# Fixing 512-row blocks of the two common experts early and running them, and the last pair of token blocks, in the wide form

## The chip, the core and the metric

The kernel runs on one core of a Trainium2 chip. The metric is device time in microseconds, from three runs of the program: 732.78, 734.6 and 736.45 us, median 734.6 us. A core has a matrix engine (PE) with its own weight loader (PEld), a vector engine (DVE), a scalar engine (ACT), a general engine (POOL) and SyncE (SP). In this kernel POOL also issues the indirect DMAs, which scatter and gather rows, and SP issues the plain DMAs.

## The reference

Three layers follow one another over 2304 tokens (4 batches of 576) of width 512, in float32.

```python
scores = where((rel >= 0) & (rel < 64), q @ k.T / 8, -1e9)      # window of 64, 8 heads of 64
x = softmax(scores) @ v                                         # 2304 x 512
h = x @ w_in                                                    # 512 -> 2048
x = (h * tanh(log1p(exp(h)))) @ w_out                           # 2048 -> 512
logits = x @ w_gate + modality_bias[modality_id]                # 8 experts
e_idx, gate_w = argmax(logits), softmax(logits)[e_idx]
out[token] = gate_w * (relu(x[token] @ w1[e_idx]) @ w2[e_idx])  # 512 -> 1024 -> 512
```

Which expert a token takes is known only when the kernel runs. With these inputs two of the eight experts get all tokens: 1168 and 1136 of the 2304. After six of the nine token blocks they hold 764 and 772.

## The kernel before

**Precision.** Each float32 matrix product is made as three products of parts: an operand is split in a high part (a rounded copy, by ACT) and a low part (the rest, a subtraction, by DVE), and high·high, low·high and high·low are summed in PSUM. So each tile of weights and of activations costs one ACT and one DVE instruction before PE can use it.

**Steps.** After a start in which the attention is alone, the main loop of `tile_kernel` runs 112 steps. A step makes one piece of hidden values (`hidden`, `hidden_wide` or `hidden_rows`) and, by `out_step(i - LAG)` with LAG = 2, the output products of the piece made two steps earlier. The text below numbers the steps from 0.

- Steps 0 to 47 are *wide* token steps. The list `WIDE = 0, 2, 4` names pairs of blocks of 256 tokens. `hidden_wide` multiplies 128 hidden columns with 512 tokens, 12 matmuls of 512 columns (L372 to L374), and `output_wide` makes 12 matmuls of 512 columns (L418 to L420). A pair takes 16 steps.
- Steps 48 to 71 are *narrow* token steps for blocks 6, 7 and 8, 8 steps each. `hidden` takes 256 hidden columns and 256 tokens: 24 matmuls of 256 columns (L356, L359, L360). `output` makes 12 matmuls of 512 columns (L407 to L409).
- Steps 72 to 103 are eight blocks of 256 rows of one expert each, 4 steps a block, narrow like the token steps. Three of them (`EARLY = 3`) are of the commonest expert and are fixed before the last tokens are routed; five (`FULL = 5`) come from a table.
- Steps 104 to 111 are two remainder slots, of 160 and of 128 rows, with `hidden_rows`. The 32 rows over 128 (`FEW = 32`) of the first are computed apart by `few_x`, `few_hidden`, `few_turn`, `few_output`, in steps 100 to 103.
- Further slots stand in conditional code at the end (`ns > 0`). With these inputs none of them runs.

**Between the layers.** A token step's hidden values pass through the activation: `mish_a` and `mish_b` on ACT and DVE, then `split_g`; an expert step's through `relu`. A finished token block is copied out of PSUM by `keep_rows`, and then routed in small tasks that are taken from a list, up to two a step: `route_logits` (DVE, L627, 16 dot products a block), `choose`, `weigh`, `place`. `place` makes five 8-column matmuls (L678 to L682), finds each row's place in a table by expert in DRAM, and scatters the 256 rows there by two indirect DMAs of POOL (L706). After four blocks `pick` finds the commonest expert; after seven, `cut` fixes its first 768 rows. After the ninth, `table` computes the slots of all other rows.

**Expert rows.** `gather` (L981, POOL) fetches 128 rows of the table, and must wait for the scatters. `turn` transposes them on PE (L1004) and splits them (ACT L1008, DVE L1009). At a block's end `finish` scales each 128 rows out of PSUM (ACT L1081) and scatters them into the output by an indirect DMA of POOL (L1082). These DMAs write the same tensor, and each one waits until the one before has landed.

**Expert weights** come by SP in pieces of 1 MB (`fetch_w`) and are split in parts of 128x1024 (`split_w1` L966 and L967, `split_w2` L974 and L975), each 1024-column part by one ACT and one DVE instruction.

**Order.** The schedule is manual: each engine runs its instructions in the order in which the code issues them, so a PE instruction that waits holds up all PE work after it, and a POOL DMA that waits holds up the gathers and scatters behind it.

Of the kernel before, what the change touches and what calls it, by code (L numbers as in the profile page):

```python
# [11 lines left out]
F32 = mybir.dt.float32  # L12
F32R = mybir.dt.float32r
BF16 = mybir.dt.bfloat16
# [38 lines left out]
EARLY = 3  # L53
# [11 lines left out]
WAIT = 1  # L65
TURN_AT = 71
NO_TASKS = 31, 47
# [217 lines left out]
class Rounds:  # L285


    def __init__(self, nc, ctx, tc, a):
        self.nc, self.tc, self.ctx = nc, tc, ctx
        self.a = a  # L290
        self.c = {}
        self.s1, self.s2, self.x01, self.home = [], [], None, None
# [219 lines left out]
    def route_consts(self):  # L512
# [67 lines left out]
        def last():  # L580
# [10 lines left out]
            nc.vector.tensor_scalar(lanes[:, FULL, 1:2], oi[:, 1:2], float(P), None, ALU.add)  # L591
# [128 lines left out]
    def pick(self):  # L720
# [3 lines left out]
        cnt = k.tile([P, NE], F32, name="cnt0")  # L724
        nc.vector.tensor_tensor(cnt, c["base"], c["r8"], ALU.subtract)
        m8 = k.tile([P, NE], F32, name="pick_m")
        i8 = k.tile([P, NE], U32, name="pick_i")
        nc.vector.max(out=m8, in_=cnt)
        nc.vector.max_index(out=i8, in_max=m8, in_values=cnt)
        c["e0i"] = i8  # L730
        c["e0"] = k.tile([P, 1], F32, name="e0")
        nc.vector.tensor_copy(c["e0"], i8[:, 0:1])
        c["first"] = k.tile([P, NE], F32, name="first")
        nc.vector.tensor_scalar(
            c["first"], c["e8"], c["e0"], float(EARLY * G), ALU.is_equal, ALU.mult
        )

        c["start"] = k.tile([P, NE], F32, name="start1")
        nc.vector.tensor_tensor(c["start"], c["r8"], c["first"], ALU.add)
        d = k.tile([P, 16], F32, name="d16")  # L740
        w = c["w16"] = k.tile([P, 16], F32, name="w16")
        nc.vector.tensor_scalar(d, c["i16"], c["e0"], None, ALU.subtract)
# [3 lines left out]
    def cut(self):  # L746

        nc, c = self.nc, self.c
        k = self.k_pool
        cnt = k.tile([P, NE], F32, name="cnt1")  # L750
        nc.vector.tensor_tensor(cnt, c["base"], c["r8"], ALU.subtract)
        nc.vector.tensor_tensor(cnt, cnt, c["first"], ALU.mult)
        n0 = k.tile([P, 1], F32, name="n0")
        nc.vector.tensor_reduce(out=n0, in_=cnt, op=ALU.add, axis=AX.X)
        nc.vector.tensor_scalar(n0, n0, 1.0 / (EARLY * G), None, ALU.mult)
        off = k.tile([P, 1], F32, name="off0")
        nc.vector.tensor_scalar(off, c["e0"], float(RCAP), float(-SENT), ALU.mult, ALU.add)
        n = 2 * EARLY
        valid = k.tile([P, n], F32, name="valid0")
        nc.vector.tensor_scalar(valid, c["lane"], n0, None, ALU.is_lt)  # L760
        t = k.tile([P, n], F32, name="idx0f")
        nc.vector.scalar_tensor_tensor(t, c["lane"], off, valid, ALU.add, ALU.mult)
        c["idx0"] = k.tile([P, n], I32, name="idx0")
        nc.vector.tensor_scalar(c["idx0"], t, float(SENT), None, ALU.add)
        nc.vector.tensor_tensor(c["base"], c["base"], c["start"], ALU.max)

    def table(self):
# [12 lines left out]
        def room(tag):  # L780
            pl = self.m_pool if tag == "y" else self.m1_pool
            t = pl.tile([P, 2 * G], F32, name="room", tag=tag)
# [12 lines left out]
        def counts():  # L795

            tmp = room("y")
# [17 lines left out]
            big = room("pq")(4 * Q * Q // 2).bitcast(BF16)  # L815
# [14 lines left out]
        def counts2():  # L830
# [27 lines left out]
            ts(at[:, 0:1], last(1), float(FULL), None, ALU.max)  # L858
# [5 lines left out]
            nc.vector.tensor_copy(q[:, :FULL], c["i16"][:, 0:FULL])  # L864
            nc.vector.tensor_copy(q[:, FULL:], at)
            nc.vector.tensor_copy(more, c["i16"][:, FULL : FULL + NSLOT - STRAIGHT])
# [4 lines left out]
            stt(has[:, 0:1], total, float(-FULL), has[:, 0:1], ALU.add, ALU.subtract)  # L871
# [5 lines left out]
        def part(lo, n, q):  # L877
# [5 lines left out]
            def experts():  # L883
                ind = st["ind"] = room("r")(n, 4 * Q + 1)
                tmp = st["tmp"] = room("pq")
# [92 lines left out]
    def gather(self, idx, i):  # L978

        r = self.row_pool.tile([P, ROW], F32, name="grow", tag=f"row{i % 2}")  # L980
# [12 lines left out]
    def gather_slot(self, s):  # L993
        idx = self.c["idx"].rearrange("p s t -> p (s t)")
        return [self.gather(idx, 2 * s + t) for t in range(1 if s == STRAIGHT - 1 else 2)]

    def turn(self, rows):
        nc = self.nc
        x = self.x_tile()
# [44 lines left out]
    def few_output(self, i):  # L1044
        nc = self.nc
        if i == 0:
            self.facc = self.acc_ps.tile([P, P], F32, name="few", tag="acc1")
# [51 lines left out]
def tile_kernel(tc, a):  # L1099
    nc = tc.nc  # L1100
    with ExitStack() as ctx:
# [22 lines left out]
        with tc.manual_schedule():  # L1124
# [144 lines left out]
            def wait_early():  # L1269
                late.extend((lambda: None,) * WAIT)  # L1270
                for s in range(EARLY):
                    rows[s] = []
                    for t in range(2):
                        late.append(lambda s=s, t=t: rows[s].append(R.gather(c["idx0"], 2 * s + t)))

            def first_slot():
                rows[EARLY] = R.gather_slot(0)
# [311 lines left out]
```

## Time and profile before

| what | value |
|---|---|
| runs, median (lowest to highest) | 734.6 us (732.78 to 736.45) |
| the profiled execution | 734.63 us, of which the span (first to last instruction) 732.8 us |
| PE busy | 710.3 us, 97% of the span |
| DVE busy | 563.4 us, 77% |
| ACT busy | 497.0 us, 68% |
| POOL busy | 153.6 us, 21% |
| granted PE clock, mean | 0.993 |

The span is 1.8 us shorter than the execution; what lies around it is in neither kernel's code. Busy time of PE is the sum of its matmuls' durations as the profile models them, with overlaps of neighbours counted once. Since a matmul's modelled duration reaches into the next one, the pace at which matmuls start is a second reading beside their duration, and the two can differ.

### The profile page before, as it was taken

Reading aid. Unit: us, or ns where it says so; the run is one execution under the profiler, and the core shown is the slowest. Engines: PE = TensorE matmul, PEld = TensorE weight load, DVE = VectorE, ACT = ScalarE, POOL = GpSimd, SP = SyncE. Lnnn points to the kernel's source line nnn. Section 1 sums busy time; section 2 is a strip of 40 time slices with the busy share of each in tenths; the row PEclk is TensorE's granted clock in tenths of the full one; section 3 lists DMA queues with packets and bytes.
Section 4 is the critical chain, followed back from the end, with each engine's and each line's share of the span. In section 5 each row is a group of like instructions: output and inputs, shape, how many; then the busy total and the mean of one; then the engine's idle time right before and its main releaser. Section 6 shows DMA issues by size and latency. Waiting matters only on the chain. (4 is left out here: it accounts for less than half of the span.)

```text
span 732.8 us, 13083 instructions
## 1 busy us (share of the span) xinstructions
PE 710.3 (97%) x4613; PEld 611.1 (83%) x4613; DVE 563.4 (77%) x1355; ACT 497.0 (68%) x1045; POOL 153.6 (21%) x292
## 2 busy tenths in 40 slices
PE   6879999999999999999999999999999999999996
PEld 5767878888888888888898899998999899999885
DVE  4879998976555479999999999998889665555562
ACT  4978888899776678777777777776322555554572
POOL 4762233232223010101101101041022112201111
PEclk9999999999999999999999999999999999999998
DMA  9986666752231331000000000360011721101350
GB/s 260 300 257 200 222 198 225 232 145 81 80 94 43 130 95 53 29 1 30 29 1 30 15 16 30 116 229 31 1 58 59 251 65 58 47 27 44 123 184 30
DMA packets 43884, 75.45 MB, mean 103 GB/s; under 512 B 3809, under 2 KB 22241, under 8 KB 43682
## 3 DMA queue, kind: packets, MB, share of 16 engines
q1 hardware_dynamic: 31842, 56.01, 24.3%
q0 software_dynamic: 4432, 14.46, 5.7%
q10 hardware_dynamic: 7536, 4.06, 1.9%
q8 instruction: 38, 0.62, 0.4%
q14 instruction: 36, 0.29, 0.1%
HBM read 82.36 MB, written 13.19 MB: 130 GB/s over the span
## 5 line engine op out<-in xcount | busy, mean ns | idle before, releaser
L627 DVE CUSTOM_DVE_ANT_0 junk<-row,wg 128x512 bf16<-128x512 f32 x144 | 99.2, 689 | 2.7
L477 ACT ACTIVATE y<-h 128x512 f32<-128x512 f32 x72 | 43.1, 598 | 55.6 <-PE h L374 32.5
L218 POOL TENSOR_SCALAR p<-p,r 128x128 f32<-128x128 f32 x144 | 68.2, 490 | 59.9 <-DVE r L211 56.2
L418 PE MATMUL acc<-w,g 128*128 128x512 f32 x192 | 77.8, 405 | 0.0
L420 PE MATMUL acc<-w,g 128*128 128x512 f32 x192 | 75.1, 391 | 0.0
L419 PE MATMUL acc<-w,g 128*128 128x512 f32 x192 | 74.8, 390 | 0.0
L504 ACT ACTIVATE g<-h 128x512 fp32r<-128x512 f32 x32 | 19.1, 598 | 80.3 <-PE h L360 80.3
L359 PE MATMUL h<-x,ew 128*128 128x256 f32 x256 | 72.6, 284 | 0.7 <-DVE x L1009 0.6
L356 PE MATMUL h<-x,ew 128*128 128x256 f32 x256 | 72.7, 284 | 0.0
L360 PE MATMUL h<-x,ew 128*128 128x256 f32 x256 | 72.4, 283 | 0.0
L488 ACT ACTIVATE pq<-pq,mid 128x512 f32<-128x512 f32 x72 | 52.3, 726 | 20.4 <-DVE pq L482 15.7
L482 DVE SCALAR_TENSOR_TENSOR pq<-y,r 128x512 f32<-128x512 f32 x72 | 49.6, 688 | 19.9 <-ACT r L480 19.3
L497 DVE TENSOR_TENSOR g<-y,g 128x512 fp32r<-128x512 f32 x72 | 49.5, 687 | 18.9 <-ACT g L496 18.7
L967 DVE TENSOR_TENSOR ew<-s,ew 128x1024 fp32r<-128x1024 f32 x32 | 39.2, 1224 | 31.8 <-ACT ew L966 31.7
L706 POOL DMA_INDIRECT xs_dram<-row,posi x18 | 18.6, 1034 | 208.4 <-DVE pq L489 69.5
L489 DVE SCALAR_TENSOR_TENSOR pq<-pq,r 128x512 f32<-128x512 f32 x72 | 50.2, 698 | 12.3 <-ACT pq L488 12.2
L407 PE MATMUL acc<-ew,g 128*128 128x512 f32 x144 | 57.9, 402 | 0.0
L408 PE MATMUL acc<-ew,g 128*128 128x512 f32 x144 | 56.4, 392 | 0.0
L409 PE MATMUL acc<-ew,g 128*128 128x512 f32 x144 | 56.2, 390 | 0.0
L478 ACT ACTIVATE y<-y,half 128x512 f32<-128x512 f32 x72 | 52.2, 725 | 2.4
L490 DVE SCALAR_TENSOR_TENSOR y<-pq,h 128x512 f32<-128x512 f32 x72 | 49.5, 687 | 3.8
L1082 POOL DMA_INDIRECT out<-out,grow x18 | 19.0, 1055 | 153.2 <-ACT out L1081 132.3
(277 smaller groups left out, 2115.3 us busy)
## 6 DMA issues: line engine op xcount, KB each, us to landing
s<-e_w SPq DMA_DIRECT2D x32, 1024.0 KB
v<-v SPq DMA_DIRECT2D x36, 256.0 KB
raw<-w_in SPq DMA_DIRECT2D x16, 512.0 KB
raw<-w_out SPq DMA_DIRECT2D x16, 512.0 KB
kt<-kT SPq DMA_DIRECT2D x17, 384.0 KB
qd<-qT SPq DMA_DIRECT2D x36, 128.0 KB
x_dram<-xs ACTq DMA_DIRECT2D x14, 256.0 KB
xraw<-x_dram SPq DMA_DIRECT2D x10, 256.0 KB
```

Of the source, the lines that this page charges most:

```text
L218: nc.gpsimd.tensor_scalar(p[:, c, :], p[:, c, :], r[:, c : c + 1], 0.0, ALU.mult, ALU.add)
L356: nc.tensor.matmul(h[:, f], w[:, 0, k, fs], xh[k], start=(k == 0), stop=False)
L359: nc.tensor.matmul(h[:, f], w[:, 0, k, fs], xl[k], start=False, stop=False)
L360: nc.tensor.matmul(h[:, f], w[:, 1, k, fs], xh[k], start=False, stop=(k == KD - 1))
L407: nc.tensor.matmul(acc[c], gh[:, 0, f, cs], w[:, 0, f], start=st, stop=False)
L408: nc.tensor.matmul(acc[c], gh[:, 0, f, cs], w[:, 1, f], start=False, stop=False)
L409: nc.tensor.matmul(acc[c], gh[:, 1, f, cs], w[:, 0, f], start=False, stop=en)
L418: nc.tensor.matmul(acc[c], gc[:, 0], w[:, 0, f], start=first, stop=False)
L419: nc.tensor.matmul(acc[c], gc[:, 0], w[:, 1, f], start=False, stop=False)
L420: nc.tensor.matmul(acc[c], gc[:, 1], w[:, 0, f], start=False, stop=last)
L488: nc.scalar.activation(p, p, AF.Square, bias=self.c["mid"][:, 0:1])
L627: nc.vector.tensor_tensor_reduce(out=junk, in0=rows[c][:, 0:D], in1=self.wg[:, e], scale=1.0, scalar=0.0, op0=ALU.mult, op1=ALU.add, accum ...
```

## The change

- Blocks 6 and 7 become a fourth wide pair (`WIDE = 0, 2, 4, 6`). Its four 512-token pieces of input are split late in step 47, as `HOMES[6]` says.
- `pick` runs twice and finds the two commonest experts. `cut` runs after block six's routing and again after all nine, and each time fixes 512 rows of both. These are four blocks of 512 rows, in the order `SLOT_EXPERT = 0, 1, 1, 0`, with a step kind of their own, "e": 8 steps a block, `hidden_wide` and `output_wide`.
- The table of slots keeps only the two remainder slots (`STRAIGHT = 2`), again of 160 and 128 rows.
- A wide block has four groups of 128 rows, and so four transposes in a block's last two steps (`turn_part`), four scalings and four output DMAs at its end. `finish` puts every other scaled piece in buffers of `x_pool`.
- Rows that wait longer are kept in `stash_pool`. The weights of both experts are fetched and split by a hand-written plan (`ADVANCE`, `experts_step`). 40 parts are split where before there were 64, since a wide block shares its weights with twice as many rows.
- The routing tasks are taken by a rate (`RATE`), one dot product as one task.

```diff
-EARLY = 3
+EARLY = 4
...
-NSLOT = 17
+NSLOT = 16
...
-STRAIGHT = 7
-FULL = 5
+STRAIGHT = 2
...
-CUT_AFTER = 6
-DOTS = 2, 2, 2, 2, 2, 2, 2, 2
+CUTS = {6: 0, NG: 1}
...
+SLOT_EXPERT = 0, 1, 1, 0
+ADVANCE = (
+    ((0, 1, 2),),
+    ((0, 2, 0),),
+    ((0, 1, 3),),
+    ((0, 2, 1), (1, 1, 0)),
+    ((0, 2, 2), (1, 1, 1)),
+    ((0, 2, 3), (1, 2, 0)),
+    ((1, 1, 2), (1, 2, 1)),
+    ((1, 2, 2),),
+)
+RATE = (0, 2), (70, 1), (72, 2), (80, 3)
...
-WIDE = 0, 2, 4
+WIDE = 0, 2, 4, 6
...
+    6: (("xraw", 0, -1, False), ("xh", 0, -1, False), ("xh", 1, -1, False), ("xl", 0, -1, False)),
...
+    def homes(self, b):
+        shape = [P, KD, 2 * G]
+        if b % 2 == 0:
+            return [self.w2_pool.tile(shape, F32R, name="ex", tag="w2") for _ in range(2)]
+        return [self.xs_pool.tile(shape, F32R, name="ex", tag=tag) for tag in ("xh", "xl")]
+
+    def turn_part(self, home, rows, t):
...
+            nc.tensor.transpose(ps[:, k], rows[:, k * P : (k + 1) * P], self.c["ident"])
+        xh, xl = (x[:, :, t * P : (t + 1) * P] for x in home)
+        nc.scalar.copy(xh, ps)
+        nc.vector.tensor_tensor(xl, ps, xh.bitcast(F32), ALU.subtract)
...
     def finish(self, acc, rows):
         nc = self.nc
         for t in range(len(rows)):
-            y = self.m_pool.tile([P, D], F32, name=f"out{t}", tag="y")
+            if t % 2:
+                y = self.x_pool.tile([P, D], F32, name=f"out{t}", tag="xraw")
+            else:
+                y = self.m_pool.tile([P, D], F32, name=f"out{t}", tag="y")
...
-            NS = EARLY + STRAIGHT
+            NS = NE_W + STRAIGHT
             steps += [("w", b, j) for b in WIDE for j in range(2 * FP)]
             steps += [("m", b, j) for b in range(WIDE[-1] + 2, NG) for j in range(FP)]
-            steps += [("s", s, k) for s in range(NS) for k in range(FS)]
+            steps += [("e", s, k) for s in range(NE_W) for k in range(2 * FS)]
+            steps += [("s", s, k) for s in range(NE_W, NS) for k in range(FS)]
...
+            def gather_early(s, t):
+                stash = s == 1 and t >= 2 or s == 3
+                idx = R.early[s // 2][:, SLOT_EXPERT[s]]
+                return R.gather(idx, t, R.stash_pool if stash else R.row_pool)
...
+                if b == 1 and j == 1:
+                    for i in range(2):
+                        R.fetch_w(e0, None, 2, i)
+                        R.fetch_w(e0, None, 1, i)
...
+                if (b, j) in ((1, 3), (2, 2)):
+                    rows[b + 1] = [gather_early(b + 1, t) for t in range(4)]
...
+                elif part == "e":
+                    xh, xl = xsp[part, b]
+                    x = [(xh[:, k], xl[:, k]) for k in range(KD)]
+                    h = R.hidden_wide(ew1[b, j // 2], j % 2, x)
...
+                if part == "e" and j >= 6 and b + 1 < NE_W:
+                    turn_two(b + 1, j - 6)
```

**Order on PE, first expert step (step 72).** In the kernel before these are the last three of its 24 hidden matmuls and the first three of its 12 output products (`x` is the turned rows, `ew` the first expert's w1 parts, `acc` and `w` the last token block's):

```order
L356 MATMUL h<-x,ew_5878 128x256
L359 MATMUL h<-x,ew_5878 128x256
L360 MATMUL h<-x,ew_5878 128x256
L407 MATMUL acc_5590<-w_1892,g 128x512
L408 MATMUL acc_5590<-w_1892,g 128x512
L409 MATMUL acc_5590<-w_1892,g 128x512
```

In the changed kernel these are the last three of its 12 hidden matmuls (`ex` is the rows' home) and the first four of the 12 output products of the last token block:

```order
L385 MATMUL h<-ex,ew_5643 128x512
L386 MATMUL h<-ex,ew_5643 128x512
L387 MATMUL h<-ex,ew_5643 128x512
L420 MATMUL acc_5390<-w_1892,g 128x512
L421 MATMUL acc_5390<-w_1892,g 128x512
L422 MATMUL acc_5390<-w_1892,g 128x512
L420 MATMUL acc_5391<-w_1892,g 128x512
```

The hidden matmuls have 512 columns instead of 256, and half as many weight loads stand between them; the output products are the same.

**Order on DVE, after the routing of block 3 (steps 51 to 53).** Before, `pick` stands in one piece (L725 to L744; `cnt` are the counts by expert, `e` the expert found), ahead of the two operations that end the hidden values of the step (L489, L490):

```order
L725 TENSOR_TENSOR cnt_4579<-base,r_3241 128x8
L728 MAX pick_m<-cnt_4579 128x8
L729 MAX_INDEX pick_i<-pick_m,cnt_4579 128x8
L732 CAST e_4585<-pick_i 128x1
L734 TENSOR_SCALAR first<-e_3237,e_4585 128x8
L739 TENSOR_TENSOR start_4589<-r_3241,first 128x8
L742 TENSOR_SCALAR d_4591<-i_3296,e_4585 128x16
L743 TENSOR_SCALAR w_4592<-d_4591 128x16
L744 SCALAR_TENSOR_TENSOR w_4592<-d_4591,w_4592 128x16
L489 SCALAR_TENSOR_TENSOR pq<-pq,r 128x512
L490 SCALAR_TENSOR_TENSOR y<-pq,h 128x512
```

Now the two picks stand each in a task of its own (L738 to L760), and the first comes after such an L502, L503 pair (L489, L490 of before):

```order
L503 SCALAR_TENSOR_TENSOR y<-pq,h 128x512
L738 TENSOR_TENSOR cnt_p_4553<-base,r_3241 128x8
L745 MAX pick_m_4555<-cnt_p_4553 128x8
L746 MAX_INDEX pick_i_4556<-pick_m_4555,cnt_p_4553 128x8
L749 CAST e_4559<-pick_i_4556 128x1
L751 TENSOR_SCALAR own_4561<-e_3237,e_4559 128x8
L753 TENSOR_SCALAR off_4563<-e_4559 128x1
L758 TENSOR_SCALAR d_4565<-i_3296,e_4559 128x16
L759 TENSOR_SCALAR w_4566<-d_4565 128x16
L760 SCALAR_TENSOR_TENSOR w_4566<-d_4565,w_4566 128x16
L495 SCALAR_TENSOR_TENSOR pq<-y,r 128x512
L510 TENSOR_TENSOR g<-y,g 128x512
```

Nine small operations ahead of the activation became nine and later seven, with L495, the activation's first multiplication, and L510, the low part of `g`, between.

**Order on POOL, after the first expert block.** Before, the scatters of block 7's tokens (`row_5551`), the two output DMAs of the first 256 rows, the scatters of block 8's tokens (`row_6130`), and the first gathers from the table:

```order
L706 DMA xs_dram<-row_5551,posi 24577x514
L704 MEMSET apart 128x1
L706 DMA xs_dram<-row_5552,posi 24577x514
L1082 DMA out<-out_6375,grow 2304x512
L1082 DMA out<-out_6380,grow 2304x512
L706 DMA xs_dram<-row_6130,posi 24577x514
L704 MEMSET apart 128x1
L706 DMA xs_dram<-row_6131,posi 24577x514
L981 DMA grow<-xs_dram,idx 128x514 x2
```

Now the four output DMAs of the first 512 rows, the scatters of block 8's tokens (`row_5881`) and the four gathers of the third block's rows, which need what was just scattered:

```order
L1126 DMA out<-out_6292,grow 2304x512
L1126 DMA out<-out_6297,grow 2304x512
L1126 DMA out<-out_6302,grow 2304x512
L1126 DMA out<-out_6307,grow 2304x512
L719 DMA xs_dram<-row_5881,posi 26625x514
L717 MEMSET apart 128x1
L719 DMA xs_dram<-row_5882,posi 26625x514
L1005 DMA grow<-xs_dram,idx_6389 128x514 x4
```

Between the first output DMA and the first gather behind it stand five other DMAs instead of three, and four of the outputs follow one another.

## Rows read from the trace of the kernel before

**Rows 1.** The page's part 1: busy time, share of the span and instructions of each engine.

```profile
PE 710.3 (97%) x4613; PEld 611.1 (83%) x4613; DVE 563.4 (77%) x1355; ACT 497.0 (68%) x1045; POOL 153.6 (21%) x292
```

**Rows 2.** Time line of PE, a wide and a narrow step: start us, us, instruction.

```profile
303.50 0.39 PE L372 MATMUL h<-xw,w 128*128 128x512 f32 x1
303.73 0.39 PE L373 MATMUL h<-xw,w 128*128 128x512 f32 x1
...
308.94 0.39 PE L372 MATMUL h<-xw,w 128*128 128x512 f32 x1
...
421.36 0.28 PE L356 MATMUL h<-x,w 128*128 128x256 f32 x1
421.48 0.28 PE L359 MATMUL h<-x,w 128*128 128x256 f32 x1
...
426.98 0.28 PE L356 MATMUL h<-x,w 128*128 128x256 f32 x1
```

**Rows 3.** Groups by line and shape, PE: busy us, mean ns, idle before.

```profile
L372 PE MATMUL h<-xw,w 128*128 128x512 f32 x128 | 51.1, 399 | 0.0
...
L356 PE MATMUL h<-x,w 128*128 128x256 f32 x160 | 45.5, 284 | 0.0
```

**Rows 4.** Windows of steps 48 to 63, 72 to 103: length, engines' busy, PEclk, DMA.

```profile
363.80:455.30 91.50, 91.17 (x592) 81.97 (x591) 85.96 (x251) 67.23 (x119) 6.10 (x9) 1.00 0.05 18
...
501.90:695.30 193.40, 192.72 (x1356) 174.31 (x1352) 129.54 (x261) 90.16 (x132) 33.86 (x33) 1.00 0.21 71
```

**Rows 5.** Time line of PE: first matmuls of steps 52 to 55; one of step 84.

```profile
386.45 0.36 PE L356 MATMUL h<-xw,w 128*128 128x256 f32 x1
...
392.47 0.36 PE L356 MATMUL h<-xw,w 128*128 128x256 f32 x1 [0.16 <-DVE y L490]
...
398.17 0.28 PE L356 MATMUL h<-xw,w 128*128 128x256 f32 x1
...
404.17 0.39 PE L356 MATMUL h<-xw,w 128*128 128x256 f32 x1 [0.18 <-DVE y L490]
...
573.48 0.39 PE L359 MATMUL h<-x,ew 128*128 128x256 f32 x1 [0.57 <-DVE x L1009]
```

**Rows 6.** Time line of DVE in step 52: the pick's first operation, what follows it.

```profile
388.90 0.16 DVE L725 TENSOR_TENSOR cnt<-base,r 128x8 f32<-128x8 f32 x1
...
390.89 0.72 DVE L489 SCALAR_TENSOR_TENSOR pq<-pq,r 128x512 f32<-128x512 f32 x1
391.64 0.69 DVE L490 SCALAR_TENSOR_TENSOR y<-pq,h 128x512 f32<-128x512 f32 x1
```

**Rows 7.** Time line of ACT, a block's end in step 106.

```profile
703.87 1.27 ACT L1081 ACTIVATE out<-acc,grow 128x512 f32<-128x512 f32 x2
705.84 0.39 ACT L387 ACTIVATE hrow<-h 128x256 f32<-128x256 f32 x1 [0.69 <-PE t L394]
```

**Rows 8.** Time line of POOL: issues of indirect DMAs.

```profile
538.31 1.00 POOL L1082 DMA_INDIRECT out<-out,grow  x1 [30.67 <-ACT out L1081]
541.84 0.99 POOL L1082 DMA_INDIRECT out<-out,grow  x1 [2.54 <-ACT g L504]
543.14 1.40 POOL L706 DMA_INDIRECT xs_dram<-row,posi  x1 [0.30 <-issue]
...
557.25 1.09 POOL L981 DMA_INDIRECT grow<-xs_dram,idx  x1 [11.44 <-DVE g L505]
558.64 1.19 POOL L981 DMA_INDIRECT grow<-xs_dram,idx  x1 [0.30 <-issue]
...
585.18 1.02 POOL L1082 DMA_INDIRECT out<-out,grow  x1 [14.98 <-ACT out L1081]
590.17 1.36 POOL L1082 DMA_INDIRECT out<-out,grow  x1 [3.96 <-DMA out<-out,grow]
```

**Rows 9.** Line L706, the scatters: from issue to landing.

```profile
DMA to landing us min/median/max: 2.9/4.0/5.3
```

**Rows 10.** Line L981, the gathers: from issue to landing.

```profile
DMA to landing us min/median/max: 3.3/3.8/8.0
```

More of the change, by code (lines that the diff above doesn't have):

```diff
@@ L728, in pick @@
         nc.vector.max(out=m8, in_=cnt)
         nc.vector.max_index(out=i8, in_max=m8, in_values=cnt)
[L730 to L739, printed above, removed]
+        c[f"e{i}i"] = i8
@@ L743, in pick, with cut @@
         nc.vector.tensor_scalar(w, d, float(NE), None, ALU.is_lt)
         nc.vector.scalar_tensor_tensor(w, d, 0.0, w, ALU.is_ge, ALU.mult)
-    def cut(self):
+    def cut(self, i, lo, hi):
         nc, c = self.nc, self.c
         k = self.k_pool
[L750 to L765, printed above, removed]
@@ new lines, in cut @@
+        cnt = k.tile([P, 3, NE], F32, name=f"cnt_c{i}")
+        n = k.tile([P, 2], F32, name=f"n{i}")
+        nc.vector.tensor_tensor(cnt[:, 2], c["base"], c["r8"], ALU.subtract)
+        for w in range(2):
+            nc.vector.tensor_tensor(cnt[:, w], cnt[:, 2], c[f"own{w}"], ALU.mult)
+        nc.vector.tensor_reduce(out=n, in_=cnt[:, 0:2], op=ALU.add, axis=AX.X)
+        lane = c["lane"][:, lo:hi]
+        start, was = k.tile([P, NE], F32, name=f"start{i}"), c["r8"]
+        for w in range(2):
+            nc.vector.scalar_tensor_tensor(
+                start, c[f"own{w}"], float(hi * P), was, ALU.mult, ALU.add
+            )
+            was = start
@@ L795, in counts @@
         def counts():
-            tmp = room("y")
+            tmp = room("row0")
             n = tmp(Q)
@@ L870, in counts2 @@
             tt(has[:, 0:1], has[:, 0:1], has[:, 1:2], ALU.add)
-            stt(has[:, 0:1], total, float(-FULL), has[:, 0:1], ALU.add, ALU.subtract)
+            tt(has[:, 0:1], total, has[:, 0:1], ALU.subtract)
             c["ns"] = k.tile([P, 1], I32, name="ns")
@@ L1380, in start_mish, with pull @@
                     mish = R.mish_a(h)
+            def pull(at):
+                if at >= len(tasks):
+                    return []
+                if isinstance(tasks[at], list):
+                    return tasks.pop(at)
+                n = [rate for first, rate in RATE if first <= i][-1]
+                now = []
+                while len(now) < n and at < len(tasks) and not isinstance(tasks[at], list):
+                    now.append(tasks.pop(at))
+                return now
             def run_tasks():
@@ L1387, in run_tasks @@
                     route_block(*waiting.pop(0))
-                now = tasks.pop(0) if tasks else []
-                if not now and waiting and waiting[0][0] < NG - 1:
+                now = pull(0)
+                if not now and waiting:
+                    at = len(tasks)
                     route_block(*waiting.pop(0))
-                    now = tasks.pop(1)
+                    now = pull(at)
                 if late:
@@ L1420, in change_x, with turn_two, split_one @@
                         xsp["m", b] = R.split_x(b == WIDE[-1] + 2)
+            def turn_two(b, half):
+                if half == 0:
+                    xsp["e", b] = R.homes(b)
+                assert len(rows[b]) == 4
+                for t in (2 * half, 2 * half + 1):
+                    R.turn_part(xsp["e", b], rows[b][t], t)
+            def split_one(s, what, k):
+                if what == 1:
+                    ew1[s, k] = R.split_w1(k)
+                else:
+                    ew2[s, k] = R.split_w2(k)
```

230 lines of the change are left out of this document (136 added, 94 removed).

## The prediction

> **What bounds the kernel now.** I read the page first: PE is busy for 97% of the span, the other engines far less [rows 1]. So what counts is how fast PE can issue its matmuls, and where it waits. For the pace I went to the time line of PE and read the starts, not the durations. In a wide step the hidden matmuls start 0.23 us apart and the next step begins 5.44 us after the last; in a narrow step they start 0.12 us apart and the step takes 5.62 us [rows 2]. The grouping by shape gives another picture: a 256-column matmul has a mean of 284 ns, a 512-column one 399 ns [rows 3]. By those means 1152 narrow matmuls would cost 327 us and 576 wide ones 230 us, a gain of 97 us. But a duration reaches beyond the next start, so the durations overlap and cannot be added; the starts decide.
>
> Then the stages. The windows of steps 48 to 63 (blocks 6 and 7) and of 72 to 103 (expert blocks) show PE busy all but 0.3 and 0.7 us, at a granted clock of 1.00, that is 2.4 GHz [rows 4]. The clock has nothing to give, and PE hardly waits. The waits that exist I looked for at step starts: steps 52, 53 and 54 take 6.02, 5.70 and 6.00 us instead of 5.62, and two of them begin or end with PE waiting for DVE's L490; one wait of 0.57 us for L1009 stands in step 84 [rows 5].
>
> **Width.** The change turns 16 token steps (48 to 63) and 32 expert steps (72 to 103) from narrow to wide. Each step does the same products. The 12 output matmuls are equal in both forms, only the hidden part differs. From the step starts [rows 2]: 5.62 - 5.44 = 0.18 us a step, 48 x 0.18 = **-8.6 us**, all of it on PE's path. Turns (72 transposes), small products for the 32 extra rows and remainder slots are as many as before: nothing.
>
> The Trainium skill, "TensorE: Matmul & The Clock Gate", section "Back-to-back issue gap", gives an isolated gap of N/2.4 + 2.5 ns. By it two 256-column matmuls take 218.3 ns and a 512-column one 215.8, which would save 2.5 ns a pair, 1.4 us in all. The rows show 0.12 and 0.23 us starts, and by whole steps 15 ns a pair, so the sum goes by the rows; the rule's result is a rival below.
>
> **Waits in the token steps.** In step 52 the routing of block 3 and `pick` stand in one piece on DVE: `pick` alone runs from 388.90 to 390.89, and only then come L489 and L490, which free the hidden values' buffer for step 53 [rows 6]. PE waits 0.16 us there [rows 5]. The three steps lose 0.86 us against 5.62, of which routing's small matmuls take some. In the changed order L502 and L503 come ahead of the pick, and the two picks are apart. This can give back 0.86 us at most; what the two smaller pieces delay is still there, so less is likely. Against it, step 47 now splits four pieces of input, not two: two more ACT and DVE operations like L490, 0.69 us each, 1.4 us if nothing hides them. What hides them is that L490's result is waited for only in the clump of step 52. I take -0.6 us, with ends of -0.9 and +1.4.
>
> **Waits in the expert steps.** The 0.57 us wait in step 84 [rows 5] comes behind a burst of weight splits in steps 82 and 83, and goes. In its place the splits for both experts lie in 24 steps (72 to 81 and 90 to 103), one or two in each; 40 parts instead of 64, at one ACT and one DVE instruction each, is less work in total. SP's fetches stand at least two steps, 10.9 us, ahead of the splits that read them, and no PE wait for a fetch shows before. New waits may come where rows are turned while weights are split, at three block ends: 3 x 0.57 - 0.57 = +1.1 as the upper end, -0.6 as the lower. I take -0.4 us.
>
> **Four outputs at a block's end.** `finish` scales four pieces on ACT instead of two, which frees PSUM for the next block: the two evictions took 1.27 us at 703.87, and the next ACT operation then waited 0.69 us for PE anyway [rows 7]. In the tail nothing changes for the last slots, but the four evictions of the last wide block stand ahead of the first slot's rows: 1.27 us more ACT, of which the 0.69 and the like hide most. I take +0.2, between 0 and +1.3.
>
> **The third block's rows.** Its gathers need block 8's scatters, and on POOL they now stand behind four output DMAs. These follow one another by landing: before, two outputs start 3.53 us apart (538.31, 541.84), or 4.99 us where weights are being fetched (585.18, 590.17); the scatter follows 1.30 later, and gathers start 1.39 apart [rows 8]. A scatter lands after 4.0 us [rows 9], a gather after 3.8 us [rows 10]. Counted from the start of step 81: the first output goes at about 4.65 (15 matmuls of 0.23, an eviction of half the 1.27 above, and half a us of latencies, an estimate), the fourth at 4.65 + 3 x 3.53 = 15.2, the scatters at 16.5 and, after the first one's own 1.40 and the small memset, about 18.2, the second lands at 22.2, the four gathers start at 22.9 to 27.1 and land at 26.7 to 30.9. PE turns the first two pieces in step 86, after 5 steps and 12 matmuls: 5 x 5.44 + 12 x 0.23 = 30.0 and 30.6, and the others 6 us later. The first pair has 3.3 and 2.5 us to spare. But four weight fetches of 1 MB start in step 81 too, and with the wider spacing (4.99) three gaps cost 4.4 us more: the first pair would be 1.1 and 1.9 us late. I take +0.7, between 0 and +2.2.
>
> **Sum.** -8.6 - 0.6 - 0.4 + 0.2 + 0.7 = -8.7. The profiled execution took 734.63 us, next to the median of 734.6, so 734.63 - 8.7 = **726.0 us**. With the terms' own ends it would be 734.63 - 10.1 = 724.5 to 734.63 - 2.6 = 732.0; the pace of a step is known to 0.02 us (two digits in the starts), 48 times that is 1 us, and runs of before lie 1.8 us apart from their median (732.78 to 736.45). I give this case 722.5 to 732.0.
>
> **Rivals.**
> 1. *The cover fails.* DVE or ACT, loaded with splits in steps that are 0.18 us shorter, becomes late for PE in many of them, as in steps 53 and 54, where a late L490 costs 0.16 to 0.38 us a step [rows 5]. In the 24 expert steps that split weights this gives 3.8 to 9.1 us back: 729.8 to 735.1, middle 732.5. For it speaks the 0.57 us wait in step 84; against it that an expert step needs one DVE operation of its own (relu's low part) and PE waits 0.7 us in all of the old expert stage [rows 4]. Chance 0.18.
> 2. *Slower: the third block's rows come late.* If the output DMAs, scatters and gathers all wait for one another's landing at 4.99 us (they share a table and POOL's queue), the second gather is the eighth of them, starts at 4.65 + 7 x 4.99 = 39.6 and lands at 43.4, 12.8 us after PE wants it at 30.6; the fourth lands at 53.4, by then wanted at 36.7 + 12.8, 3.9 us more. PE would stand still for 16.7 us in place of the 0.7 of the sum: 726.0 + 16.0 = 742.0. It decides the sign once the rows are 9.4 us late (8.7 + 0.7). Against it: gathers started 1.39 us apart, with no wait for landing [rows 8]. Chance 0.06.
> 3. *A pair of narrow matmuls is no slower.* If the 0.18 us a step belongs to the stage and not to the form (the wide steps read all lie before 364 us, the narrow ones after), and two narrow matmuls take what a wide one takes, the width term is nothing and the others add to -0.1: 734.5 us, no change. The rule of the Trainium skill, "Back-to-back issue gap", comes close to this rival; by it the time would be 733.1. Against it, the rows show the gap inside the hidden part: two starts of 0.12 are more than one of 0.23 [rows 2]. Chance 0.03.
> 4. *It does not do what it says.* If some rows do not fit four blocks and two remainder slots, a conditional slot runs: fetch, split and 8 steps with nothing to hide behind, some 45 us (an estimate: four steps of 5.62 and their rows and weights one after the other), about 771. The counts, 764 and 772 after six blocks and at least 1136 in the end, leave 144 and 112 rows, which fit. Chance 0.03.
>
> **How the numbers follow.** The main case has 0.70. What a measurement of this kernel can tell from no change is about 0.5%, 3.7 us: faster means under 730.9. Faster: main case 0.70, and a third of the first rival, 0.06: 0.76. Same: the rest of the first rival, 0.12, and the third, 0.03: 0.15. Slower: the second and the fourth, 0.09. The range must reach into the first rival: 722.5 to 733.0 holds the main case and two thirds of it, about 0.82.
>
> **What the profile will show.** Steps 48 to 63 and 72 to 103 should start 5.44 us apart, the stage of steps 48 to 63 should last about 88 us instead of 91.5, that of 72 to 103 about 188 instead of 193.4. In the means by shape the gain will look ten times greater. PE's waits for DVE in steps 51 to 55 should shrink. In step 86 the wait for the gathers' rows should be under 2 us. I am wrong if wide expert steps take more than 5.5 us, if PE waits for weight splits between steps 72 and 103, or if a fourth output of a block starts more than 13 us after its first.

## The result, and the profile after

The changed kernel takes 726.13 us (median of 6 runs, 724.87 to 727.7), the kernel before 734.51 us (median of 6, 732.32 to 736.8): a ratio of 0.9883, with a 95% interval of 0.9857 to 0.9909. Run again later beside other kernels it took 725.87 us against 733.66, a ratio of 0.9892 (0.9873 to 0.9911).

The page's part 1 of the changed kernel (busy time, share, instructions) stands against [rows 1]:

```profile
PE 699.7 (97%) x4037; PEld 578.3 (80%) x4037; DVE 538.9 (75%) x1348; ACT 474.6 (66%) x1021; POOL 152.9 (21%) x292
```

PE has 576 matmuls fewer and is busy for 97% as before. The pace is read from the starts again. The time line of PE in the changed kernel, the first matmuls of step 73 and the first of step 74 (start us, us, instruction), against [rows 2]:

```profile
501.73 0.39 PE L385 MATMUL h<-ex,ew 128*128 128x512 f32 x1
501.95 0.39 PE L386 MATMUL h<-ex,ew 128*128 128x512 f32 x1
502.18 0.39 PE L387 MATMUL h<-ex,ew 128*128 128x512 f32 x1
...
507.17 0.39 PE L385 MATMUL h<-ex,ew 128*128 128x512 f32 x1
```

An expert step now takes 5.44 us, with 0.23 us between starts. The windows of steps 48 to 63, 64 to 71, 72 to 103 and 104 to the end (length, busy us of PE, PEld, DVE, ACT, POOL, then PEclk), against [rows 4]:

```profile
361.50:449.30 87.80, 87.80 (x401) 72.23 (x400) 81.58 (x243) 66.33 (x116) 6.24 (x9) 1.00 0.04 16
449.30:496.20 46.90, 46.90 (x311) 42.76 (x309) 39.10 (x97) 35.74 (x62) 9.02 (x9) 1.00 0.41 141
496.20:685.20 189.00, 187.09 (x971) 153.11 (x968) 114.55 (x299) 66.40 (x105) 30.95 (x32) 1.00 0.35 119
685.20:723.20 38.00, 30.56 (x189) 26.89 (x187) 16.13 (x23) 19.08 (x34) 7.37 (x7) 0.94 0.29 100
```

Steps 48 to 63 went from 91.5 to 87.8 us, and PE never waits in them. Steps 72 to 103 went from 193.4 to 189.0, and here PE waits for 1.9 us where it waited 0.7. The rest is about as long as before (46.6 to 46.9, and 37.5 to 38.0). From step 48 on that is 7.4 us. The profiled span is 9.6 us shorter; the other 2.3 us lie before step 48, where both kernels issue the same matmuls. The first matmul of step 48 starts at 363.83 us in the kernel before and at 361.51 in the changed one, whose profiled run (724.87 us) is the lowest of its six. In ten more profiles of kernels alike up to there it is between 362.9 and 365.8 us, so this part is the scatter of the program's start and not the change. One of the ten is the changed kernel again: step 48 starts at 363.60 us there, and what follows is 8.0 us shorter than in the kernel before.

Where PE waits in steps 72 to 103 is seen in step 86, which took 8.45 us where step 87, with the same work, took 6.33. The time line of PE there, from the first matmul of step 86 to the first of step 87, shows the transposes of the third block's rows waiting for their gathers:

```profile
575.26 0.39 PE L385 MATMUL h<-ex,ew 128*128 128x512 f32 x1
...
579.18 0.63 PE L1033 MATMUL t<-ident,grow 128*128 128x128 f32 x4 [1.03 <-DMA grow<-xs_dram,idx]
580.51 0.63 PE L1033 MATMUL t<-ident,grow 128*128 128x128 f32 x4 [0.71 <-DMA grow<-xs_dram,idx]
...
583.71 0.39 PE L385 MATMUL h<-ex,ew 128*128 128x512 f32 x1
```

And POOL's time line shows why they come late (against [rows 8]):

```profile
552.39 1.00 POOL L1126 DMA_INDIRECT out<-out,grow  x1 [23.57 <-ACT out L1125]
555.92 1.86 POOL L1126 DMA_INDIRECT out<-out,grow  x1 [2.53 <-ACT ew L998]
564.29 0.98 POOL L1126 DMA_INDIRECT out<-out,grow  x1 [6.51 <-DMA out<-out,grow]
567.79 0.98 POOL L1126 DMA_INDIRECT out<-out,grow  x1 [2.52 <-DMA out<-out,grow]
569.08 0.97 POOL L719 DMA_INDIRECT xs_dram<-row,posi  x1 [0.30 <-issue]
...
575.58 0.97 POOL L1005 DMA_INDIRECT grow<-xs_dram,idx  x1 [4.27 <-DVE room L942]
```

The four outputs start 3.5, 8.4 and 3.5 us apart. The long gap is one output's landing (from 555.92 to 563.52 us), and in it SP's time line has two weight fetches of 1 MB:

```profile
556.94 0.37 SPq L984 DMA_DIRECT2D s<-e_w  x1
557.52 0.37 SPq L979 DMA_DIRECT2D s<-e_w  x1
```

The row of the gather names DVE's table work (L942) as its releaser, though its data come from the scatters. The experiments decide between the two.

### The profile page after: what moved, and what is told of

Its sections match the earlier page's. It is cut to its first block, busy times and chain, and to the rows that moved or that the text cites. A ratio compares the mean times of both kernels' runs of the same rounds, so it can differ in the third digit from the quotient of the medians.

```text
span 723.2 us, 11805 instructions
## 1 busy us (share of the span) xinstructions
PE 699.7 (97%) x4037; PEld 578.3 (80%) x4037; DVE 538.9 (75%) x1348; ACT 474.6 (66%) x1021; POOL 152.9 (21%) x292
## 5 line engine op out<-in xcount | busy, mean ns | idle before, releaser
L431 PE MATMUL acc<-w,g 128*128 128x512 f32 x256 | 102.7, 401 | 0.0
L433 PE MATMUL acc<-w,g 128*128 128x512 f32 x256 | 100.1, 391 | 0.0
L432 PE MATMUL acc<-w,g 128*128 128x512 f32 x256 | 99.8, 390 | 0.0
L490 ACT ACTIVATE y<-h 128x512 f32<-128x512 f32 x72 | 43.1, 598 | 56.7 <-PE h L387 49.6
L385 PE MATMUL h<-xw,w 128*128 128x512 f32 x192 | 76.3, 398 | 0.0
L387 PE MATMUL h<-xw,w 128*128 128x512 f32 x192 | 75.0, 390 | 0.0
L386 PE MATMUL h<-xw,w 128*128 128x512 f32 x192 | 74.9, 390 | 0.0
L495 DVE SCALAR_TENSOR_TENSOR pq<-y,r 128x512 f32<-128x512 f32 x72 | 49.6, 689 | 24.0 <-ACT r L493 22.5
L510 DVE TENSOR_TENSOR g<-y,g 128x512 fp32r<-128x512 f32 x72 | 49.4, 687 | 18.3 <-ACT g L509 18.3
L518 DVE SCALAR_TENSOR_TENSOR g<-h,g 128x512 fp32r<-128x512 f32 x32 | 22.1, 689 | 53.5 <-ACT g L517 53.5
L502 DVE SCALAR_TENSOR_TENSOR pq<-pq,r 128x512 f32<-128x512 f32 x72 | 50.2, 697 | 13.9 <-ACT pq L501 13.8
L433 PEld LDWEIGHTS acc<-w,g 128*128 128x128 f32 x256 | 48.0, 188 | 10.7
L432 PEld LDWEIGHTS acc<-w,g 128*128 128x128 f32 x256 | 48.2, 188 | 9.2
L431 PEld LDWEIGHTS acc<-w,g 128*128 128x128 f32 x256 | 48.1, 188 | 9.0
L503 DVE SCALAR_TENSOR_TENSOR y<-pq,h 128x512 f32<-128x512 f32 x72 | 49.5, 687 | 2.9
L431 PE MATMUL acc<-ew,g 128*128 128x512 f32 x128 | 50.9, 398 | 0.0
```

The costliest lines, as they stand in the source:

```text
L385: nc.tensor.matmul(h, w[:, 0, k, fs], xh, start=(k == 0), stop=False)
L386: nc.tensor.matmul(h, w[:, 0, k, fs], xl, start=False, stop=False)
L387: nc.tensor.matmul(h, w[:, 1, k, fs], xh, start=False, stop=(k == KD - 1))
L431: nc.tensor.matmul(acc[c], gc[:, 0], w[:, 0, f], start=first, stop=False)
L432: nc.tensor.matmul(acc[c], gc[:, 0], w[:, 1, f], start=False, stop=False)
L433: nc.tensor.matmul(acc[c], gc[:, 1], w[:, 0, f], start=False, stop=last)
```

## The experiments

Step lengths below are from one hidden group's first matmul to the next one's, as in [rows 5]. Most kernels are the changed kernel with one edit; `before_pick_apart` is the kernel before with one edit, and `best` has two. `quarters`, `one_pick`, `before_pick_apart` and `splits_twice` were run once, so there the steps in the trace are read and not small differences of the time.

**Outputs without an order among them** (no_order). The tracker of dependencies is told that the outputs of a block write different rows:

```diff
...
+            for x in sent:
+                self.tc.declare_no_dep(got.ins, x.ins, reason="each token has a row of its own")
+            sent.append(got)
```

> The changed kernel, but the four output DMAs of a block do not wait for one another (each row of the output belongs to one token). Theory: the 2.1 us that step 86 takes longer (8.45 us against 6.33 in step 87) is the wait for the third block's rows, whose scatters stand behind four outputs that follow one another by landing (starts at 552.39, 555.92, 564.29, 567.79). Without that order the outputs start about 1.3 us apart, the scatters about 11 us earlier, the gathers by 571 instead of 575.58, step 86 takes about 6.35 us, and the time falls by 2.1 us to about 724.0. Rival: the first gather at 575.58 waits for DVE's table work (L942, which ends at 575.59 and is what the row names), not for the scatters: then it stays at 575.6, step 86 stays at 8.4 and the time at 726.

Measured: 723.43 us (722.68 to 727.7), ratio to the kernel before 0.9866 (0.9821 to 0.9911). POOL's time line:

```profile
553.77 1.00 POOL L1127 DMA_INDIRECT out<-out,grow  x1 [23.57 <-ACT out L1126]
555.07 0.99 POOL L1127 DMA_INDIRECT out<-out,grow  x1 [0.30 <-ACT out L1126]
556.37 0.98 POOL L1127 DMA_INDIRECT out<-out,grow  x1 [0.30 <-ACT jexp L683]
557.66 1.50 POOL L1127 DMA_INDIRECT out<-out,grow  x1 [0.30 <-issue]
559.46 0.97 POOL L719 DMA_INDIRECT xs_dram<-row,posi  x1 [0.30 <-DVE cnt_c L768]
...
568.92 0.97 POOL L1005 DMA_INDIRECT grow<-xs_dram,idx  x1 [7.21 <-DVE room L890]
```

The first matmuls of steps 86 and 87, and DVE's L942:

```profile
576.64 0.39 PE L385 MATMUL h<-ex,ew 128*128 128x512 f32 x1
...
583.02 0.39 PE L385 MATMUL h<-ex,ew 128*128 128x512 f32 x1
...
576.81 0.16 DVE L942 TENSOR_TENSOR room<-lanes,room 128x4 f32<-128x4 f32 x1
```

The outputs start 1.3 us apart, the first gather at 568.92, and step 86 takes 6.38 us. The gather starts 8 us before L942, and its row now names L890: the row names a DVE instruction that ended nearby. What the gather follows is the second scatter, by 0.9 us after its landing here (568.03), in the changed kernel (574.70) and in the next run (571.56). So the rival with the table work falls, and the 2.07 us of step 86 (8.45 - 6.38) are the chain of outputs and scatters. It is the step that shows this: in this run and the next the interval of the time overlaps that of the changed kernel.

**The second half of the weights fetched later** (fetch_late). SP first reads a word of the last gathered row:

```diff
-                if b == 1 and j == 1:
-                    for i in range(2):
-                        R.fetch_w(e0, None, 2, i)
-                        R.fetch_w(e0, None, 1, i)
+                if b == 1 and j in (1, 4):
+                    i = j // 4
+                    if i:
+                        word = rows[2][3][0:1, D + 1 : D + 2].bitcast(I32)
+                        nc.values_load(word, engines=[SP], min_val=0, max_val=NT)
+                    R.fetch_w(e0, None, 2, i)
+                    R.fetch_w(e0, None, 1, i)
```

> The changed kernel, but SP reads one word of the last gathered row of the third block before it fetches the second half of the first expert's weights (two DMAs of 1 MB, at 556.94 and 557.52 in the changed kernel). Theory: these two fetches made the second output DMA land 7.6 us after its issue (555.92 to 563.52) instead of 2.8; without them the third output starts at about 559.5 instead of 564.29, the gathers at about 570.8 instead of 575.58, step 86 takes about 6.35 us, time about 724.0. Rival: the outputs are slow by themselves or the gathers wait for DVE's L942: step 86 stays at 8.4, time 726. A cost is possible where the late fetches themselves stand in a wait of the splits in steps 94 and later: none expected, there are 40 us between.

Measured: 724.26 us (723.45 to 724.91), ratio 0.9864 (0.9833 to 0.9894). POOL's time line:

```profile
553.97 1.00 POOL L1126 DMA_INDIRECT out<-out,grow  x1 [23.57 <-ACT out L1125]
557.50 1.86 POOL L1126 DMA_INDIRECT out<-out,grow  x1 [2.54 <-ACT ew L998]
561.91 0.98 POOL L1126 DMA_INDIRECT out<-out,grow  x1 [2.54 <-DMA out<-out,grow]
565.42 0.98 POOL L1126 DMA_INDIRECT out<-out,grow  x1 [2.53 <-DMA out<-out,grow]
...
572.44 0.97 POOL L1005 DMA_INDIRECT grow<-xs_dram,idx  x1 [3.50 <-DVE room L924]
```

The first matmuls of steps 86 and 87:

```profile
576.84 0.39 PE L385 MATMUL h<-ex,ew 128*128 128x512 f32 x1
...
583.22 0.39 PE L385 MATMUL h<-ex,ew 128*128 128x512 f32 x1
```

With the order among the outputs kept and only the fetches moved, the gaps are 3.5, 4.4 and 3.5 us, and step 86 again takes 6.38. So both are needed for the wait: four outputs in a row, and two fetches in the middle of them.

**Two narrow matmuls for each wide one** (halves). In the 32 expert steps only; `hidden_parts`, not shown, makes each hidden product of 512 tokens as two of 256:

```diff
-                    h = R.hidden_wide(ew1[b, j // 2], j % 2, x)
+                    h = R.hidden_parts(ew1[b, j // 2], j % 2, x, 2)
```

> The changed kernel, but in the 32 expert steps each hidden matmul of 512 columns is made as two of 256, everything else as it is. This measures the width term alone. Theory (starts of steps in the kernel before): 5.62 us a step instead of 5.44, 32 x 0.18 = 5.8 us slower, about 731.9; in step 86 the wait for rows shrinks by the 0.9 us that steps 81 to 85 are longer, so 731.0 to 731.9. Rival one, width costs nothing and the gain of the change belonged to the stage: 726. Rival two, by the mean durations (284 against 399 ns): 384 x 0.169 = 65 us slower, 791. The Trainium skill, TensorE: Matmul & The Clock Gate, section Back-to-back issue gap, gives N/2.4 + 2.5 ns: 2.5 ns a pair, 1 us in all, about 727.

Measured: 730.57 us (729.8 to 732.48), ratio to the kernel before 0.9947 (0.9923 to 0.9971). PE's time line, from the first matmul of step 73 to the first of step 74:

```profile
504.07 0.28 PE L399 MATMUL h<-ex,ew 128*128 128x256 f32 x1
504.18 0.28 PE L400 MATMUL h<-ex,ew 128*128 128x256 f32 x1
504.30 0.28 PE L401 MATMUL h<-ex,ew 128*128 128x256 f32 x1
...
509.69 0.28 PE L399 MATMUL h<-ex,ew 128*128 128x256 f32 x1
```

Plain steps take 5.62 us again, 0.18 more than wide ones, with nothing else changed. The median is 4.4 us above that of the changed kernel. In the profiles, steps 72 to 103 took 192.8 us where the changed kernel's first profile has 189.0, though step 86 waits 0.96 us less (7.49 us instead of 8.45), since its rows are wanted later. The other 31 steps took 4.8 us more, against 31 x 0.18 = 5.6 worked out. Half of the difference is step 74, whose wait for a split went (5.69 us instead of 5.90); the rest is in steps that do more than the plain ones, where the two forms lie less than 0.18 us apart (step 78: 6.51 and 6.39 us). The rivals (nothing; 1 us; 65 us) are out.

**Four matmuls of 128 columns** (quarters). The same edit with 4 in place of 2.

> As halves, but each hidden matmul of 512 columns is made as four of 128. Theory: a straight line through the two starts in the kernel before (120.8 ns at 256 columns, 226.7 at 512: 0.414 ns a column and 14.9 ns a matmul) gives 67.9 ns at 128 columns; 384 x (4 x 67.9 - 226.7) = 17.2 us slower, about 743; step 5.98 us. Rival: with so few columns the weight load, one for each matmul, sets the pace: more than 67.9 ns a matmul, steps over 6.0 us. The Trainium skill, TensorE: Matmul & The Clock Gate, section Back-to-back issue gap, gives a sustained 81 ns for 128 columns with weight loads, which would be 37 us slower, about 763.

Measured: 809.45 us in one run, 83 us above the changed kernel where the straight line gave 17 and the other estimate 37. PE's time line:

```profile
599.80 0.28 PE L401 MATMUL h<-ex,ew 128*128 128x128 f32 x1
599.91 0.27 PE L399 MATMUL h<-ex,ew 128*128 128x128 f32 x1
600.02 0.28 PE L400 MATMUL h<-ex,ew 128*128 128x128 f32 x1
```

Matmuls of 128 columns start 0.11 us apart, nearly as slowly as those of 256 (0.12). The granted clock is 1.00 in that stretch. So the straight line through two sizes does not go on to 128 columns: these float32 matmuls, with a weight load of 128x128 each, stay at 111 ns. PEld's loads follow each other at the same 0.11 us in that stretch, which fits the rival with the weight load, but no run changes the load alone. It is not a pace for every pair of load and matmul: the five matmuls of 8 columns in `place`, in bf16 and with a load of 128x128 each, start 0.02 to 0.04 us apart in the kernel before (L678 to L682, 386.31 to 386.43 us).

**The pair of blocks 6 and 7 back in the narrow form** (pair_narrow).

```diff
-NO_TASKS = 31, 47, 63
-WIDE = 0, 2, 4, 6
+NO_TASKS = 31, 47
+WIDE = 0, 2, 4
...
```

> The changed kernel with blocks 6 and 7 back in the narrow form (WIDE = 0, 2, 4), the expert stage as changed. Theory: 16 x 0.18 = 2.9 us slower by the width, and whatever of the waits in steps 51 to 55 belonged to the narrow form's input splits comes back (0 to 0.9): 729.0 to 729.9. Rival: the pair form saved the waits rather than the width, or its four input pieces cost what the width gives: 726 to 727.

Measured: 727.91 us (727.0 to 728.46), ratio 0.9919 (0.9895 to 0.9942): 2.0 above the changed kernel of the same chip, where 2.9 or more was expected. Steps 48 to 63 took 90.60 us, 2.82 more than the 87.78 of the changed kernel, as worked out, and steps 52 to 55 had no waits. But step 86 took 6.38 us: here block 8's rows are scattered ahead of the outputs (at 550.30 and 551.95 us, the first output at 558.33), so its wait, 1.4 us in the changed kernel's profile beside it, is gone too. The expectation had left that out. From step 48 on this profile is 1.3 us longer than that one; the rest of the 2.0 is within the scatter of the start. The 0.88 us between 91.48 (the kernel before) and 90.60 is what the narrow token steps had lost to waits.

**The picks in one piece** (one_pick). Both in the routing task of block 3, as the one pick stood before:

```diff
-                    tasks.extend(([R.pick], [lambda: R.pick(1)]))
+                    tasks[-1] += [R.pick, lambda: R.pick(1)]
```

> The changed kernel with both picks in the routing task of block 3, in one piece on DVE ahead of the activation's two operations, as the one pick stood before. Theory: the piece of some 3.3 us (2.0 for the first, two thirds of it for the second) makes L503 late, PE waits at the start of step 53 and in its neighbours, 0.9 us or more in steps 52 to 55, where the changed kernel has 0.1 (steps of 5.55, 5.44, 5.44, 5.44); 727 us. Rival: the waits of before came from the two input splits that stood in steps 54 and 55 (L458), not from the pick: no wait, 726.

Measured: 728.61 us in one run. Steps 48 to 63 took 89.39 us instead of 87.78. The first matmul of step 53 in PE's time line:

```profile
392.59 0.50 PE L385 MATMUL h<-xw,w 128*128 128x512 f32 x1 [1.32 <-DVE y L503]
```

So one piece on DVE of routing and picks is enough to make L503 late, in this form too. It is a longer piece than before: two picks, 3.1 us, where the one pick took 2.0.

**The same part alone, in the kernel before** (before_pick_apart).

```diff
-                    tasks[-1].append(R.pick)
+                    tasks.append([R.pick])
```

> The kernel before with one part of the change alone: the pick in a task of its own, not behind the routing of block 3 in one piece. Theory: with the blocks 6 and 7 still narrow, the waits of steps 52 to 55 go, as pair_narrow showed them gone (steps 48 to 63 took 90.6 us there, 91.5 in the kernel before, 87.8 in the changed one): 90.6 us for steps 48 to 63, 0.9 us less in all, 733.7. Rival: the waits belonged to other work of DVE that the change also moved (the dot products of the next block, taken in fixed pairs here): steps 52 to 55 keep 0.5 us or more above 5.62, 91.2 us or more.

Measured: 735.87 us in one run beside 734.39 of the kernel before. Steps 48 to 63 took 90.61 us, as expected, with steps 52 to 55 at 5.70, 5.62, 5.62, 5.62. The two input splits (L458) are still among them, so the waits were not theirs. The end was not 0.9 us earlier: the later routing tasks all moved by one place, steps 64 to 71 took 46.0 instead of 46.6 us, and steps 72 to 103 took 194.2 instead of 193.4, most of it in step 72 (6.75 instead of 6.07). From step 48 on the profile is 0.7 us shorter; one run's time cannot show that.

**Twice the low parts** (splits_twice). DVE makes the low part of each weight part a second time, in `split_w1` and in `split_w2`.

```diff
         nc.scalar.copy(t[:, 0], src)
-        nc.vector.tensor_tensor(t[:, 1], src, t[:, 0].bitcast(F32), ALU.subtract)
+        for _ in range(2):
+            nc.vector.tensor_tensor(t[:, 1], src, t[:, 0].bitcast(F32), ALU.subtract)
```

> The changed kernel, but DVE makes the low part of each of the 40 weight parts twice (the second time the same numbers), 40 x 1.13 = 45 us more work on DVE, one or two operations of 1024 columns more in each of the 24 steps that split. This measures the cover of the wide expert steps. Theory: DVE has room there: in steps 80 to 103 PE waits for DVE nowhere by more than 0.3 us; only in steps 72 to 79, where the routing of the last block and the splits of two experts come together (DVE busy 6 to 7 us as the profile adds it, in steps of 5.44 to 6.39), waits appear, up to 2 us in sum; 726 to 728. Rival (the cover is thin): 0.16 to 0.38 us in each of the 24 steps, in steps 80 to 103 too, 3.8 to 9.1 us: 730 to 735.

Measured: 749.32 us in one run, 23 us more than the changed kernel. The waits of PE from step 48 on (engine, line, for whom: us in total, times, longest):

```profile
PE h L386 <- DVE ex L1038: 4.2, 1, 4.2
PE h L397 <- DVE x L1052: 3.6, 1, 3.6
PE acc L432 <- DVE ew L1001: 3.4, 2, 2.5
PE t L1035 <- DVE ex L1038: 2.2, 1, 2.2
PE t L691 <- DVE ex L1038: 2.1, 1, 2.1
PE acc L422 <- DVE g L410: 1.8, 1, 1.8
...
```

Steps 81 to 103 are as long as in the changed kernel to 0.01 us, but for step 86: there the cover is ample, as the theory had it. Steps 71 to 80, though, took 17.2 us more (steps 79 and 80: 10.47 and 12.38 us instead of 6.34 and 5.44), against the 2 us expected, and the slots from step 104 on 5.6 us more. So where the last block's routing and the splits of both experts meet, hardly any is left: the plan splits some 15 parts there, and 15 extra operations of 1.13 us are 17 us, about what these steps lost. Which operation made which wait was not followed one by one.

**A version that is faster than both** (best). Outputs without order, and two entries of the split plan exchanged, so that step 74 finds its w2 part:

```diff
-    ((0, 1, 2),),
-    ((0, 2, 0),),
+    ((0, 2, 0),),
+    ((0, 1, 2),),
```

> The changed kernel without the order among a block's four outputs (as in no_order, which took step 86 from 8.45 to 6.38 us) and with the first w2 part of the first expert split one step earlier, in step 72 instead of 73 (two entries of the split plan exchanged). In the changed kernel step 74 takes 5.90 us, with PE waiting for DVE's L999 at 510.44. Theory: step 86 is 6.35 us and step 74 is 5.44 us, together -2.5 us: 723.6, and 2.5 below the changed kernel on the same chip. Rival: the split that now comes later (w1, L991) is late for step 76, or the fetch that landed at 500.17 is too late for step 72 and holds ACT: then a step between 72 and 76 gains a wait of like size and only the 2.1 us remain.

and beside it the changed kernel again (after_again):

> The changed kernel itself, once more, as the measure on the same chip for the runs beside it. 726.1 us as at first; step 86 again 8.4 us, the steps 48 to 63 again 5.44 us each but for the three routing places; the start of step 48 may differ by 1 or 2 us from 361.51, since five profiles with the same instructions up to there have it between 361.5 and 363.8.

Measured: 724.08 us (723.69 to 724.77), ratio to the kernel before 0.9872 (0.985 to 0.9895); the changed kernel beside it 725.87 (725.2 to 726.36). The two ranges do not meet, 1.8 us apart in the middle, where 2.5 was expected. In the profile step 74 took 5.44 instead of 5.89 us and step 86 6.38. In this profile of the changed kernel step 86 took 7.75 and not 8.45, so the wait there is 1.4 to 2.1 us from one run to the next: the first gather follows the second scatter by 4.1 us here and by 5.2 in the first profile. What is left of PE's waits from step 48 on is one row:

```profile
PE h L397 <- DVE x L1050: 0.4, 1, 0.4
```

## Why the prediction was right, point by point

The forecast was 726.0 us, the time 726.13. That they agree to 0.13 us is luck: the forecast difference was 8.7 us, the medians differ by 8.4 and, run again later, by 7.8, and the profiles from step 48 on by 7.4 and 8.0. The terms one by one, from the two first profiles and the runs that undid them:

| term | forecast | measured |
|---|---|---|
| width, 48 steps | -8.6 | -2.8 (steps 48 to 63, undone in pair_narrow) and 0.18 us a plain expert step, -5.8 for 32 (halves gave back 4.8 in 31 of them) |
| waits in the token steps | -0.6 | -0.9 (91.48 to 90.60 with the picks apart) |
| waits in the expert steps | -0.4 | -0.7 (0.8 of step 84 gone, 0.46 new in step 74, -0.4 spread over other steps) |
| four outputs, tail | +0.2 | +0.4 (the 0.4 us that PE waits for L1050 in step 108) |
| third block's rows | +0.7 | +2.1 and +1.4 in two profiles |
| steps 64 to 71 | no term | +0.3 (46.55 to 46.89) |
| sum | -8.7 | -7.4 from step 48 on in the first profile |

**Width** was right, and by the reading that counts: step starts. PE's busy time fell by 10.6 us, while the means by shape would have given 97.

**The picks** were right in mechanism. Two experiments turned it both ways: apart, the waits are gone in the kernel before; together, they come back in the changed one at 1.6 us.

**The four outputs in the tail** were right in mechanism. ACT scales four pieces one after the other, 2.43 us instead of 1.27, and no longer waits for PE behind them. Counted from the step's start, the splits that follow come 0.3 us later, and with them the low part of the last slot's rows (L1050):

```profile
693.68 2.43 ACT L1125 ACTIVATE out<-acc,grow 128x512 f32<-128x512 f32 x4
...
700.96 0.39 PE L397 MATMUL h<-ew,x 128*128 128x256 f32 x1 [0.43 <-DVE x L1050]
```

**The third block's rows** are the step that was mis-sized. The chain was named rightly, from outputs through scatters to gathers, and so was the weights' traffic in it. The value, 0.7, was chosen in the lower half of 0 to 2.2, though the text itself had the fetches start in that very step and had worked out that the pieces would then come 1.1 and 1.9 us late; step 86 measured 2.1 us, 1.7 of it in the rows of its waits. The shape was off too. Not four fetches start in step 81: two had started at 540.51 and 541.08 us, in step 79, and two start at 556.94 and 557.52, in step 82. And there are not three gaps of 4.99 us, but one of 8.4 between two of 3.5, because both fetches fall on one output. Their sum (15.4 us from the first output to the fourth) is the same as 3 x 4.99 = 15.0 within half a us, and passes the 13 us that the prediction had named as a sign that it was wrong. (The 4.65 us for the first output add up to 4.6 from their parts; the first profile has 4.56.) The prediction came out close all the same, since the term was 1.4 us too small at most and the others miss by less.

**The new wait for a split** (step 74, L999, 0.17 us by the row, 0.46 by the step) was another sign named there; it is real, small, and gone in the faster version. So two of the prediction's three signs of being wrong came true, and cost 0.5 and 2.1 us; the third, wide expert steps over 5.5 us, did not, since plain ones took 5.44.

**The rivals.** The late rows as a mechanism that would make it slower did not come to that: gathers start 1.3 us apart and do not wait for each other's landing. The failing cover did not happen, but splits_twice shows that it was nearer than the text allowed for in steps 71 to 80. That a narrow pair costs no more is disproved by halves: 15 ns a pair. The rule of the Trainium skill ("TensorE: Matmul & The Clock Gate", section "Back-to-back issue gap"), 2.5 ns a pair, does not agree with that, and the measurement decides. No conditional slot ran.

What stays open is where the start before step 48 gets its scatter: the two first profiles differ by 2.3 us there, later ones scatter by as much, and nothing was tried on it. Open too are the -0.4 us spread over the expert steps and the +0.3 of steps 64 to 71, where the rows are now turned in steps 70 and 71.

## What to carry to other kernels

Where matmuls are pipelined, price a change of their shape by the distance of starts between whole steps, not by the mean duration of one: here the means said 97 us and the starts 8.6, and the starts were right. When a block becomes larger, look at what its end now sends out in a row: four outputs that follow each other by landing are harmless alone and became a wait when two fetches of 1 MB fell between them. A releaser that a row names can be only an event that ended nearby; where two candidates end together, move one of them and look again.

## What was not expected of the hardware

With float32 operands, a weight load of 128x128 for each matmul and a granted clock of 1.00, matmuls of 128 columns start 0.11 us apart, those of 256 columns 0.12, those of 512 columns 0.23. So making a matmul of 512 columns into two costs 7% (15 ns of 227), and into four 96% (444 ns instead of 227, in one run): going from 256 to 128 columns saves next to nothing of a matmul's time.
